# A fused sliding-window attention and gated MLP: plain values loaded once, masks and first keys reordered, plain scores in one visit

## The chip, the cores and the metric

The kernel runs on one core of a Trainium2 chip. The metric is the device time of one execution, in microseconds (us). Before the change the median of four runs is 305.04 us (304.75 to 305.53). One of the executions was taken by the hardware profiler; its own time is 304.69 us.

## The reference

Inputs are q, k and v of shape 8 x 8 x 576 x 64 (batch, head, position, width) and the weights of an MLP: w_in 512 x 2048, w_out 2048 x 512 and beta of 2048. The computation, cut to what matters:

```python
rel = pos[:, None] - pos[None, :]
plain = (rel >= 0) & (rel < 32)                       # heads 0 to 3
dil = (rel >= 0) & (rel < 128) & (rel % 4 == 0)       # heads 4 to 7
attn = softmax(where(mask, q @ k.T / 8, -1e9))
x = concat_heads(attn @ v).reshape(4608, 512)
h = x @ w_in
out = (h * sigmoid(beta * h)) @ w_out
```

So half of the heads attend to the last 32 positions ("plain"), the other half to every fourth of the last 128 ("dilated").

## The kernel before, in words

**Two kinds of work on TensorE.** Attention runs batch by batch (b = 0 to 7), the MLP token tile by token tile (nine tiles of 512 tokens). Per tile there are 16 blocks of h (L811: four matmuls of 512 columns each, then tanh on ScalarE at L820 and the product on VectorE at L825), and four blocks of output (L846: 16 matmuls each, taken in parts of four). Attention of batch b is laid between the MLP matmuls of earlier tiles, because tile t needs the attention of its tokens first.

**The planner.** No order is written by hand. Each step is an `Op` with the engines that may do it, estimated durations, what it depends on and a due number `vt`; `Plan.run` walks through time, and for each engine takes, among the steps that could start within a few tens of ns of the earliest one (`NEAR`), the one with the smallest `vt`. It also hands out the eight PSUM banks: a `Group` of a kind holds a bank until its last reader is done, and `CAPS` says how many a kind may hold (h 3, p 4, o 2, z 4, a 8, s 5). Where PE would stand idle for over 300 ns of planned time it puts in a filler matmul (L958, on zeros). The instruction streams of the engines are fixed by this plan; on the chip each engine follows its own stream in order.

**Plain scores.** The 576 queries of a head are cut into six blocks of 96; a block needs 128 keys (32 before it and its own 96). Two heads sit in the two halves of the 128 partitions, so one matmul uses 64 rows (L673). For batches 0 and 1 a visit to these 64-row matmuls covers one head pair x and half of the blocks (steps S00, S10, S01, S11: 6 matmuls, two banks); from batch 2 on two head pairs together (12 matmuls, four banks, `PAIRED`). An exponential on ScalarE (L576) writes the bank to `pt` (288 columns), and, from batch 1 on, a product with a 0/1 mask on VectorE or GpSimd (L580) zeroes what lies outside the window. In batch 0 the mask is added in PSUM instead: inside the same step the matmuls L631 (dilated, 512 columns) or L661 and L664 (plain) put 0 or -65536 into the bank, and the scores add to it. Values are multiplied at L729, from `pt` and `vp`.

**Plain values.** `vp` holds for each of the 24 blocks all 128 keys with their values, so the 32 rows that two neighbouring blocks share are loaded twice: per batch one DMA of 128 x 24 x 64 (three DMAs for batch 0), issued by GpSimd at L384.

**Loads.** GpSimd issues all loads that change float32 to bf16. At the start these are in order: keys and queries of the dilated heads of batch 0, keys and queries of the plain heads, `vd` (dilated values), `vp` (plain values), then w_in in three chunks of 512, 512 and 1024 columns, the tail values `vt`, keys and queries of batch 1, w_out in two halves and so on. For batches 0 to 2 keys and queries are transposed on TensorE (L448 dilated, L455 plain) and copied out of PSUM (L232); from batch 3 on by DMA transposes that SyncE issues. SyncE's first DMA is `beta_row`, 8 KB. The vector w of halved beta is built by a small transpose (L894).

**Masks.** GpSimd builds them with memsets and affine selects: `add_d`, `add_P`, `add_F` early, `mask_d`, `maskn_PP` and `maskn_FP` (128 x 384 each) later.

Of the kernel before, what the change touches and what calls it, by code (L numbers as in the profile page):

```python
# [22 lines left out]
class Op:  # L23
    def __init__(self, engs, fn, deps, vt, acquire, group, dma, lat, halves=False, sbuf=False):
        self.halves, self.sbuf = halves, sbuf
        self.engs, self.fn, self.vt, self.acquire = engs, fn, vt, acquire
        self.deps = [d for d in deps if d is not None]
        self.dma, self.lat, self.group = dma, lat, group
        self.end = self.ready = None
        self.waits = 0  # L30
        self.next = []
        for g in group if isinstance(group, list) else [] if group is None else [group]:
            g.users.append(self)


class Plan:
# [3 lines left out]
    CAPS = {"h": 3, "p": 4, "o": 2, "z": 4, "a": 8, "s": 5}  # L40
    SWITCH = 95
    LAT = {"PE": 210, "ACT": 45, "DVE": 45, "POOL": 60, "SP": 0}
# [5 lines left out]
    def op(self, engs, fn, deps=(), vt=0.0, acquire=None, group=None, dma=0, lat=None, halves=False, sbuf=False):  # L48
        acquire = acquire if acquire is None or isinstance(acquire, list) else [acquire]
        o = Op(engs, fn, deps, vt, acquire, group or acquire, dma, lat, halves, sbuf)  # L50
        self.ops.append(o)
        return o

    def run(self, filler=None, filler_until=0.0):
# [36 lines left out]
        while n_left:  # L91
# [21 lines left out]
            for e, c in near.items():  # L113
                first = min(s for s, _, _ in c)
                s, o, d = min((x for x in c if x[0] <= first + self.NEAR[e]), key=lambda x: (x[1].vt, x[0]))
                picks.append((s, o.vt, e, o, d))
# [58 lines left out]
def kernel(  # L175
# [38 lines left out]
    APART = 4  # L214

# [26 lines left out]
    mask_n = {n: const([P, 2, 2, QT], BF16, f"maskn_{n}") for n in ("FP", "PP")}  # L242
# [12 lines left out]
    pt = [const([P, NI * 2, P], BF16, f"pt{x}") for x in range(2)]  # L255
# [52 lines left out]
    def t_fill2(e):  # L308
        for x in range(2):
            nc.vector.memset(pt[x][:, :, QT:P], 0.0)  # L310
        nc.vector.memset(ptt[:], 0.0)
    fill2 = plan.op([("DVE", 1500)], t_fill2, vt=-7.9)

    def t_fill3(e):
        nc.vector.memset(vp[0][:, :, D:D + 1], 1.0)
        nc.vector.memset(vp[0][0:WIN, 0, 0:D], 0.0)
# [55 lines left out]
    def first_rows(m):  # L372
        nc.gpsimd.memset(m[0:WIN, 0], 0.0)
    for i, n in enumerate(("PP", "FP")):
        def t_mask_n(e, n=n):
            band(mask_n[n][:].rearrange("p a b n -> p (a b) n"), [[0, 4]], [(1, QT)], WIN, -1, 1.0, 0.0)
            if n == "FP":
                first_rows(mask_n[n])
        late_mask("n" + n, 1900, t_mask_n, -7.183 + .001 * i)
# [17 lines left out]
    def plain_v(b, p0, c0):  # L397
        return bass.AP(tensor=v.tensor, offset=v[b, 0].offset + (p0 - WIN) * D + c0 * QT * D,
                       ap=[[D, P - WIN if p0 else WIN if c0 == 1 else P], [QT * D, 4 * NI - c0], [1, D]])

    def direct_vp(b, deps, vt):
        if b:
            return [load("POOL", (vp[b % 2][:, :, 0:D], plain_v(b, 0, 0)), deps, vt, 768, .27, 1450,
                         1100 if b < DIRECT else 4000)]
        half = 2 * NI
        return [load("POOL", (vp[0][WIN:P, 0:half, 0:D], plain_v(0, WIN, 0)[:, 0:half]), deps, vt, 288, .25),
                load("POOL", (vp[0][0:WIN, 1:half, 0:D], plain_v(0, 0, 1)[:, 0:half - 1]), deps, vt, 92, .25),
                load("POOL", (vp[0][:, half:, 0:D], plain_v(0, 0, half)), deps, vt, 384, .27)]

    def direct_vd(b, deps, vt, tdeps=()):  # L410
        src = v[b, 4:8].rearrange("h (t T) d -> t h (T d)", T=C)[0:P]
        out = [load("POOL", (vd16_of[b].rearrange("p h T d -> p h (T d)"), src), deps, vt, 512, .35)]
        for c in range(2):
            src = bass.AP(tensor=v.tensor, offset=v[b, 4].offset + ((P - WIN) * C + c) * D,
                          ap=[[2 * D, 2 * KTL], [S * D, 4], [1, D]])
            out.append(load("POOL", (vt_[b % 2][:, c, :, 0:D], src), list(tdeps), vt + (1.245 if b == 0 else .02 if b < DIRECT else 0) + .001 + .001 * c, 96, .2))
# [26 lines left out]
    def t_transposes(g, z, kind, i):  # L443
# [6 lines left out]
        else:  # L450
            tp = bank(g, BF16)[:, 0:S].rearrange("p (j g) -> p j g", j=RP)
            for j in range(RP):
                for h in range(2):
                    rows = slice(64 * h, 64 * h + 64)
                    nc.tensor.transpose(tp[rows, j], stp[z][rows, i, j * D:(j + 1) * D], ident_b[rows, rows])  # L455

# [49 lines left out]
    def attention(b, ld, names, vts):  # L506
# [4 lines left out]
        if b < DIRECT:  # L511
            for n in [x for x in names if x[0] in "KQ"]:
# [3 lines left out]
                src = ld["qk", z, 0 if kind == "P" else 4]  # L516
                tr = plan.op([("PE", (18 * mm(64) if kind == "P" else 6 * mm(QT)))],
                             lambda e, g=g, z=z, kind=kind, i=i: t_transposes(g, z, kind, i),
                             [src, ident], vt, acquire=g)
# [40 lines left out]
        vdeps["P", 1] = [ld["vp"][-1], (fill3, fill4)[kv]]  # L560
        vdeps["P", 0] = (ld["vp"][:-1] or ld["vp"]) + [(fill3, fill4)[kv]]
# [11 lines left out]
        def exp_and_mask(key, sop, g, vt, n, sc, w, m, tiles):  # L573
# [4 lines left out]
            if b >= ADDED or key == ("T",):  # L578
                def mask(e):
                    E[e].tensor_tensor(out=w(), in0=w(), in1=m(), op=ALU.mult)  # L580
                ex = plan.op([("POOL", 170 + 2.2 * n), ("DVE", 160 + .8 * n)], mask,
                             [ex] + ([mask_tail] if key == ("T",) else [mask_ops["D"]] if key[0] >= 2 else
                                     [mask_ops["n" + ("PP" if key[1] else "FP")]]), vt, sbuf=True)
# [17 lines left out]
        for name in [n for n in names if n[0] in "ST"]:  # L601
# [24 lines left out]
            if x >= 2:  # L626

                def score(e, xs=xs, gs=gs):
                    if b < ADDED:
                        for g in gs:  # L630
                            nc.tensor.matmul(  # L631
                                bank(g).rearrange("p (a n) -> p a n", a=4), lhsT=ident_b[:],
                                rhs=add_d[:].unsqueeze(1).to_broadcast([P, 4, P]), start=True, stop=False)
                    for n, x in enumerate(xs):
                        for i in range(4):
                            r, h4 = i // 2, 2 * (x - 2) + i % 2
                            for c in range(2):
# [5 lines left out]
                sop = plan.op([("PE", len(xs) * 4 * mm(P) + (190 + 2 * mm(4 * P) if b < ADDED else 0))], score,  # L643
                              deps + ([ident, adds["D"]] if b < ADDED else []), vt, acquire=gs, halves=True)
# [9 lines left out]
            j = int(name[2])  # L654

            def score(e, xs=xs, j=j, gs=gs):
                if b < ADDED:
                    for g in gs:
                        lo = 0
                        if j == 0:  # L660
                            nc.tensor.matmul(bank(g)[:, 0:QT], lhsT=ident_b[:], rhs=add_p["F"][:],  # L661
                                             start=True, stop=False)
                            lo = 1
                        nc.tensor.matmul(  # L664
                            bank(g)[:, lo * QT:3 * QT].rearrange("p (a n) -> p a n", n=QT), lhsT=ident_b[:],
                            rhs=add_p["P"][:].unsqueeze(1).to_broadcast([P, 3 - lo, QT]),
                            start=j == 1, stop=False)
                for n, x in enumerate(xs):
                    for a in range(3):
                        i = 3 * j + a  # L670
                        for h in range(2):
# [4 lines left out]
            sop = plan.op([("PE", len(xs) * 3 * mm(QT) + (190 + 2 * mm(3 * QT) if b < ADDED else 0))], score,  # L676
                          ([o for x in xs for o in steps[f"KP{x}"] + steps[f"QP{x}"]] if b < DIRECT else ready["P"])
                          + ([ident, adds["P"]] if b < ADDED else []), vt, acquire=gs, halves=True)
# [3 lines left out]
            for n, x in enumerate(xs):  # L682
                for h in range(2):
# [4 lines left out]
                                 lambda j=j: mask_n["PP" if j else "FP"][:].rearrange("p a b n -> p (a b) n")[  # L688
                                     :, (0, 1)[j == 0]:(0, 1)[j == 0] + 3],
                                 [("pt", x, i) for i in range(3 * j, 3 * j + 3)])  # L690
        for name in [n for n in names if n[0] in "VU"]:
# [33 lines left out]
            def values(e, x=x, j=j, g=g):  # L725
                pv = bank(g)[:, 0:6 * (D + 1)].rearrange("p (m h e) -> p m h e", m=3, h=2)
                for a in range(3):
                    for h2 in range(2):
                        nc.tensor.matmul(pv[:, a, h2, :], lhsT=pt[x][:, (3 * j + a) * 2 + h2],  # L729
                                         rhs=vp[kv][:, (2 * x + h2) * NI + 3 * j + a, 0:D + 1],  # L730
                                         start=True, stop=True)
            vop = plan.op([("PE", 6 * mm(D + 1))], values,
                          [sdone[x, j, 0], sdone[x, j, 1]]
                          + vdeps["P", x], vt, acquire=g)
            used(("vp", kv), vop)
            for i in range(3 * j, 3 * j + 3):
                used(("pt", x, i), vop)
# [135 lines left out]
    for n, (z, h0) in enumerate(((0, 4), (1, 4), (0, 0), (1, 0))):  # L873
        ld[0]["qk", z, h0] = direct_qk(0, z, h0, [], -9 + .01 * n)
# [27 lines left out]
    vts[first.index("T"):len(first)] = [-.5, -.4, -.3, -.2]  # L902
# [89 lines left out]
```

## Time and profile before

| what | before |
|---|---|
| median of 4 runs | 305.04 us |
| the profiled execution: its time, its span | 304.69 us, 302.8 us |
| PE busy | 293.1 us, 97% |
| VectorE, ScalarE, GpSimd busy | 183.5, 170.9, 90.5 us |
| matmuls with w_in (L811) and w_out (L846) | 138.3 and 139.4 us busy |
| packets of DMA on GpSimd's queue | 66672, 66.1% of the engines' span |
| granted TensorE clock | 0.999 |

The span is the time from the first to the last instruction in the profile, and the execution's own time is 1.89 us longer. Busy PE time counts the filler matmuls too, and the ends of matmuls are modelled, so that two groups of matmuls can overlap in the listing: what a group costs is read from its start to the start of the next group. In the listing by time each row gives start, duration, engine, line, operation, output and inputs, the number of instructions, and in square brackets how long the engine was idle before it and what released it.

### The profile page before, as it was taken

How to read it: one execution, taken by the hardware profiler on the slowest of the kernel's cores; microseconds unless marked ns; L12 is line 12 of the kernel's file. 1: busy time of each engine (PE TensorE's matmuls, PEld its weight loads, DVE VectorE, ACT ScalarE, POOL GpSimd, SP SyncE). 2: the span in 40 equal slices, each digit the busy share in tenths (PEclk: the TensorE clock that was granted, in tenths of full speed). 3: DMA queues.
4: the chain of work that ended last, by engine and by line, in shares of the span. 5: the costliest groups of instructions: out<-in, count | busy, mean ns of one | idle time of the engine just before them, and what ended most of it. 6: DMA issues, size and time to landing. Idle time of an engine off the chain costs nothing.

```text
span 302.8 us, 5999 instructions
## 1 busy us (share of the span) xinstructions
PE 293.1 (97%) x2275; PEld 148.4 (49%) x2312; DVE 183.5 (61%) x424; ACT 170.9 (56%) x314; POOL 90.5 (30%) x131
## 2 busy tenths in 40 slices
PE   7899999999999999999999999999999999999995
PEld 5565545554544444445444444444444444444454
DVE  3568874987866746886676658756764343343300
ACT  2767963877547645765664557555664544554311
POOL 8988562836045106320470055100000000000000
PEclk9999999999999999999999999999999999999999
DMA  6999999999999997999899989996132100100122
GB/s 101 178 210 203 206 184 210 195 128 168 193 181 209 158 209 156 174 122 234 150 165 183 185 185 151 164 191 169 56 93 75 38 35 35 37 35 35 55 83 73
DMA packets 117376, 42.47 MB, mean 140 GB/s; under 512 B 93748, under 2 KB 110916, under 8 KB 117348
## 3 DMA queue, kind: packets, MB, share of 16 engines
q0 software_dynamic: 66672, 19.66, 66.1%
q1 hardware_dynamic: 50532, 22.36, 37.8%
q8 instruction: 18, 0.29, 0.4%
q10 hardware_dynamic: 144, 0.07, 0.1%
q14 instruction: 10, 0.08, 0.1%
HBM read 39.32 MB, written 18.87 MB: 192 GB/s over the span
## 4 chain that ended last, share of the span: by engine, by line
PE 80%; DMA 12%; DVE 3%; issue 2%; POOL 1%; ACT 1%; POOLq 0%; SPq 0%; DVEq 0%
PE bank L846 39%; PE bank L811 34%; DMA vd<-in_v_dram 4%; DMA dk<-s 3%; DMA st<-in_q_dram 2%; PE bank L729 2%; DMA s<-in_k_dram 2%; DVE g L825 1%; PE bank L673 1%; PE bank L639 1%; PE bank L714 1%; POOL st L384 1%; PE bank L699 0%; DVE xdm L596 0%; PE bank L780 0%
## 5 line engine op out<-in xcount | busy, mean ns | idle before, releaser
L846 PE MATMUL bank<-w_out_bf,g 128*128 128x512 bf16 (+2 forms) x587 | 139.4, 367 | 1.7 <-issue 0.8
L825 DVE SCALAR_TENSOR_TENSOR g<-tnh,bank 128x512 bf16<-128x512 bf16 x144 | 97.8, 685 | 70.8 <-ACT tnh L820 69.8
L820 ACT ACTIVATE tnh<-bank,beta_half 128x512 bf16<-128x512 f32 x144 | 98.4, 689 | 72.5 <-PE bank L811 67.0
L811 PE MATMUL bank<-xT,w_in_bf 128*128 128x512 bf16 (+1 forms) x568 | 138.3, 376 | 0.9 <-issue 0.2
L811 PEld LDWEIGHTS <-w_in_bf 128*128 128x128 bf16 x584 | 55.1, 98 | 61.0 <-issue 0.2
L846 PEld LDWEIGHTS <-g 128*128 128x128 bf16 x608 | 54.5, 98 | 55.4
L861 ACT ACTIVATE osb<-bank 128x512 f32<-128x512 f32 (+1 forms) x35 | 20.6, 588 | 31.6 <-PE bank L846 31.3
L576 ACT ACTIVATE pt<-bank 128x288 bf16<-128x288 f32 x64 | 21.5, 418 | 6.3 <-PE bank L673 6.2
L576 ACT ACTIVATE ptd<-bank 128x512 bf16<-128x512 f32 x32 | 16.9, 603 | 7.0 <-PE bank L639 7.0
L596 DVE TENSOR_TENSOR xsp<-bank,rcp 96x384 bf16<-96x384 f32 x32 | 17.7, 554 | 1.1
L384 POOL DMA_DIRECT2D vp<-in_v_dram x10 | 18.0, 1800 | 0.5 <-PE bank L455 0.5
L924 POOL COPY pace<-xT 1x2 bf16<-1x2 bf16 x4 | 0.7, 176 | 58.3 <-DMA xT<-x 58.3
L595 DVE RECIPROCAL rcp<-bank 128x4 f32<-128x4 f32 (+2 forms) x72 | 12.9, 179 | 5.3 <-PE bank L729 3.9
L580 DVE TENSOR_TENSOR ptd<-ptd,mask_d 128x512 bf16<-128x512 bf16 x27 | 12.0, 453 | 6.1 <-ACT ptd L576 4.9
L596 DVE TENSOR_TENSOR xdm<-bank,rcp 128x256 bf16<-128x256 f32 x32 | 13.6, 425 | 1.1
L384 POOL DMA_DIRECT2D vt<-in_v_dram x16 | 13.8, 1048 | 0.0
L384 POOL DMA_DIRECT2D s<-in_q_dram x10 | 13.7, 1370 | 0.0
L729 PEld LDWEIGHTS <-pt 128*128 128x128 bf16 x192 | 9.0, 97 | 5.8 <-POOL pt L580 0.6
L384 POOL DMA_DIRECT2D s<-in_k_dram x10 | 11.2, 1121 | 1.2 <-issue 1.2
L232 POOL COPY vd<-st 128x1024 bf16<-128x1024 bf16 x5 | 5.2, 1036 | 19.0 <-DMA st<-in_v_dram 15.1
L729 PE MATMUL bank<-vp,pt 128*128 128x65 bf16 x192 | 10.1, 193 | 0.1
L863 DVE TENSOR_SCALAR osb<-bank 128x512 f32<-128x512 f32 (+2 forms) x3 | 1.4, 469 | 13.3 <-PE bank L846 13.3
(107 smaller groups left out, 182.7 us busy)
## 6 DMA issues: line engine op xcount, KB each, us to landing
out_dram<-osb SPq DMA_DIRECT2D x35, 256.0 KB, 3.0
s<-in_k_dram POOLq DMA_DIRECT2D x10, 288.0 KB, 6.5
s<-in_q_dram POOLq DMA_DIRECT2D x10, 288.0 KB, 9.4
vp<-in_v_dram POOLq DMA_DIRECT2D x7, 384.0 KB, 18.2
w_out_bf<-in_moe_w_out_dram POOLq DMA_DIRECT2D x2, 1024.0 KB, 16.4
st<-in_k_dram POOLq DMA_DIRECT2D x6, 288.0 KB, 13.1
st<-in_q_dram POOLq DMA_DIRECT2D x6, 288.0 KB, 12.5
x<-xsp SPq DMA_DIRECT2D x12, 144.0 KB
```

Of the source, the lines that this page charges most:

```text
L232: (nc.scalar.copy if e == "ACT" else E[e].tensor_copy)(out=out, in_=in_)
L384: {"POOL": nc.gpsimd, "SP": nc.sync}[queue].dma_start(out=out, in_=in_)
L576: nc.scalar.activation(out=w(), in_=sc(), func=ACT.Exp, scale=SCALE)
L580: E[e].tensor_tensor(out=w(), in0=w(), in1=m(), op=ALU.mult)
L595: nc.vector.reciprocal(out=r, in_=p[..., D])
L596: nc.vector.tensor_tensor(out=dst, in0=p[..., 0:D], in1=r.unsqueeze(len(p.shape) - 1).to_broadcast(list(p.shape[:-1]) + [D]), op=ALU.mult)
L729: nc.tensor.matmul(pv[:, a, h2, :], lhsT=pt[x][:, (3 * j + a) * 2 + h2], rhs=vp[kv][:, (2 * x + h2) * NI + 3 * j + a, 0:D + 1], start=True ...
L811: nc.tensor.matmul(bank(g)[:, a:z], lhsT=w_in_bf[:, kt, fb * P:(fb + 1) * P], rhs=xT[:, kt, xo + a:xo + z], start=(i == 0 and kt == kts[0] ...
L820: nc.scalar.activation(out=th[:, 0:n], in_=bank(g)[:, 0:n], func=ACT.Tanh, scale=beta_half[:, fb:fb + 1])
L825: nc.vector.scalar_tensor_tensor(out=g_t[t % 2][:, fb, c0:c0 + n], in0=th[:, 0:n], scalar=1.0, in1=bank(g)[:, 0:n], op0=ALU.add, op1=ALU.mult)
L846: nc.tensor.matmul(bank(g)[:, lo:hi], lhsT=g_t[t % 2][:, fb, tb * P:(tb + 1) * P], rhs=w_out_bf[:, fb, lo:hi], start=(fb == 0), stop=(fb = ...
L861: nc.scalar.mul(out=ob[:, lo:hi], in_=bank(g)[:, lo:hi], mul=0.5)
```

## The change

Seven edits:

1. `vp` is loaded without the doubled rows: 96 x 24 x 64 per batch into partitions 32 to 127 (two DMAs for batch 0), and the 32 shared rows are copied inside SBUF by VectorE or GpSimd (`halo`: one copy of 32 x 4 x 5 x 64 per batch, two halves for batch 0). The rows that have no predecessor are zeroed once.
2. The additive masks of batch 0 become steps of their own, `added`, which take the banks; the scores follow later.
3. The dilated keys of batch 0 are loaded by SyncE as float32 into the unused `g_t[1]`, and ScalarE and VectorE cast one half each.
4. From batch 3 on all plain scores of a batch are one visit: 24 matmuls into six banks of a new kind "w", six exponentials of 384 columns instead of eight of 288, and six mask products.
5. `maskn_PP` and `maskn_FP` become one `mask_n` of 128 x 864.
6. `vt` of batch 0 and the tail steps of batch 0 get later due numbers.
7. `NUDGE`: 29 steps, by their number, get a bias in ns that shifts the start time by which the planner compares them (it does not shift the step itself).

```diff
+    CAPS = {"h": 3, "p": 4, "o": 2, "z": 4, "a": 8, "s": 5, "w": 6}
+    NUDGE = {75: 400, 116: -150, 160: -150, 200: -400, 206: -900, 210: 400, 221: 60, 240: -60, 250: -150,
...
-                first = min(s for s, _, _ in c)
-                s, o, d = min((x for x in c if x[0] <= first + self.NEAR[e]), key=lambda x: (x[1].vt, x[0]))
+                first = min(s + o.bias for s, o, _ in c)
+                s, o, d = min((x for x in c if x[0] + x[1].bias <= first + self.NEAR[e]), key=lambda x: (x[1].vt, x[0]))
...
+        o = load("SP", (stage, src), [], -9.1, 576, .41, 400, 1200)
+        return [plan.op([("ACT", 175 + .834 * RD * D), ("DVE", 160 + 1.042 * RD * D)],
+                        lambda e, x=x: copy(e, std[0][:, x], stage[:, x]), [o], -9.1, sbuf=True) for x in range(2)]
...
+            o = load("POOL", (vp[b % 2][WIN:P, hs.start * NI:hs.stop * NI, 0:D], src), deps, vt, n * 144, .27,
+                     1150 if b else 750, 1100 if b < DIRECT else 4000)
+            def halo(e, hs=hs):
+                copy(e, rows[0:WIN, hs, 1:NI, 0:D], rows[QT:P, hs, 0:NI - 1, 0:D])
...
+                before = [plan.op([("PE", 2 * mm(4 * P))], added, [ident, adds["D"]], vt, acquire=gs)] if b < ADDED else []
...
+            if b >= AT_ONCE:
+                gs = [Group("w") for _ in range(6)]
...
+                sop = plan.op([("PE", 2 * NI * mm(QT))], score, [o for x in range(2) for o in steps[f"KP{x}"] + steps[f"QP{x}"]]
+                              if b < DIRECT else ready["P"], vt, acquire=gs, halves=True)
...
-    vts[first.index("T"):len(first)] = [-.5, -.4, -.3, -.2]
+    vts[first.index("T"):len(first)] = [.2,.35,.45,.5]
```

In the built programs the streams change as follows. Both have the same matmuls apart from fillers: 35 before, 29 after. TensorE: the four L631 matmuls now stand ahead of the first transposes; the transposes of the plain keys of batch 1 (2 x 18) stand ahead of the first h block, where before they came after the eleventh h block; the runs of 64-row matmuls (transposes L455 and scores, with nothing else between) are 29 instead of 30: five fewer in batches 3 to 7, two more in batch 1, two more in batch 2. GpSimd: the first DMA is now the dilated queries; the plain keys of batch 1 are loaded before the second and third chunk of w_in instead of after. VectorE: both copies of qT of batch 0 and two halo copies stand ahead of the first normalisation (L595); ScalarE casts its half of the keys first, and has two copies of kT of batch 1 ahead of its last xT copy of batch 0. The last 100 output matmuls are the same.

## The prediction

> **What bounds the kernel now.** The first page is read first: TensorE (PE) is busy for 97% of the span. That includes fillers, so the next view is the list of instructions by time. I read it by the distance from the start of one group to the start of the next; the durations themselves overlap.
>
> ```profile
> 1.13 4.43 PE L958 MATMUL bank<-zero 128*128 128x256 bf16 x22 [1.13 <-DVE warm L290]
> 6.06 0.68 PE L448 MATMUL bank<-ident_b,st 96*128 96x96 bf16 x12 [0.50 <-DMA st<-in_k_dram]
> 7.59 0.67 PE L448 MATMUL bank<-ident_b,st 96*128 96x96 bf16 x12 [0.30 <-DVE dk L232]
> ...
> 9.11 0.60 PE L631 MATMUL bank<-add_d,ident_b 128*128 128x512 bf16 x2 [0.41 <-DVE dq L232]
> 9.65 0.40 PE L639 MATMUL bank<-dq,dk 64*128 64x128 bf16 x8
> 9.98 0.76 PE L455 MATMUL bank<-ident_b,st 64*64 64x64 bf16 x36
> 11.36 0.76 PE L455 MATMUL bank<-ident_b,st 64*64 64x64 bf16 x36 [0.63 <-DMA st<-in_q_dram]
> 12.71 0.43 DVE L232 COPY vd<-vd 128x1024 bf16<-128x1024 bf16 x1 [1.18 <-DMA vd<-in_v_dram]
> 13.02 1.08 ACT L576 ACTIVATE ptd<-bank 128x512 bf16<-128x512 f32 x2
> 13.91 0.18 DVE L595 RECIPROCAL rcp<-bank 128x4 f32<-128x4 f32 x1 [0.77 <-PE bank L714]
> 20.14 4.88 PE L811 MATMUL bank<-xT,w_in_bf 128*128 128x512 bf16 x28
> ```
>
> The reader is to see three phases in the first 20 us. Until 11.4 PE waits for loads: keys at 6.06, queries 1.5 us later, the plain queries at 11.36. From 13 to 20.7 it is paced by ScalarE (back to back from 10.08 to 15.8) and VectorE (from 13.91 to 19.9). Then h runs. Lost PE time before the first h block at 18.36: 1.13, 4.93 (to 6.06), 1.01 (6.58 to 7.59), 1.01 (8.10 to 9.11), 0.69 (36 transposes take 1.38 at 9.98, but 0.69 at 11.36), 0.12 of filler, and 0.9 in pieces of 0.1 to 0.24 between 14.3 and 18.2: 9.8 us in all, of which about 6 are the wait for the first load.
>
> The same reading from 18.4 to 60 us gives 1.9 us lost: 0.40 of filler at 24.85, 0.5 at L699 (8 matmuls take 0.75 at 26.18, 0.24 at 48.15), 0.30 and 0.11 around 32, 0.15 at 33.3, 0.26 at 39.8, 0.2 at 56.4. After 60 us four matmuls of 512 columns take 0.86 us again and again; one wait of 0.3 us at 71 is left. So after 60 us only the cost of changing between 128-row and 64-row matmuls can be saved:
>
> ```profile
> 67.40 1.03 PE L846 MATMUL bank<-w_out_bf,g 128*128 128x512 bf16 x4
> 68.36 0.43 PE L673 MATMUL bank<-qT,kT 64*128 64x96 bf16 x12
> 68.72 1.04 PE L846 MATMUL bank<-w_out_bf,g 128*128 128x512 bf16 x4
> 69.59 1.03 PE L811 MATMUL bank<-xT,w_in_bf 128*128 128x512 bf16 x4
> ```
>
> The four ahead of the visit take 0.96 instead of 0.86: 0.10 to enter. Twelve score matmuls take 0.36, six (at 34.51) take 0.24: 0.02 each and 0.12 to leave. A visit costs 0.22 us beyond its work.
>
> **The parts.** All against the profiled execution (304.69, span 302.8).
>
> *Additive masks ahead.* The two L631 pairs take 0.54 each (9.11 to 9.65, 12.05 to 12.59). They move into the wait for the keys: `add_d` is ready at 5.72 now, and one GpSimd issue of 0.79 less stands ahead of it, so about 4.9. The four take 0.86 there, where five of 22 fillers go. That is 1.1 us off PE between 9 and 12.6. All four dilated exponentials can now run before the plain queries are there; today the second pair starts at 13.02. The L661 and L664 masks stay where they are, at 0.04 to 0.17 each.
>
> *Keys by SyncE.* SyncE issues at 0.81, GpSimd at 1.36 with 0.79 per issue. By window, the DMA engines are busy 0.01 of the first 2 us, 0.25 from 2 to 3, 0.78 from 3 to 4: there is room. The queries become GpSimd's first load. They land no earlier than today's first load (6.05) and no later than today (7.54): 0 to 1.5 us for all that follows on that queue. I take 1.0, since the room ahead of 4 us is about one load. The keys themselves: no load of this size stands on SyncE's queue; the nearest rows are a 256 KB store, 3.0 us to landing, and today's first load, 4.7 us, so 3.8 to 5.5; plus the casts (0.64 us on ScalarE and 0.76 on VectorE for 576 elements, by 768/576: 0.85 and 1.0) they are ready at 4.8 to 6.5 against 6.06. Both engines idle there. If they come at 6.5, the queries come next anyway.
>
> A rule speaks against this edit: the Trainium skill, "DMA: Bandwidth & Descriptors", section "Issuing engines are not separate DMA queues", says that issuing from several engines saves only the issuing time, because all queues share the same 16 DMA engines. By it this part would give about 0.8 us, the one issue, and not 1.0; the windows above show the shared engines idle at that time, which the rule doesn't speak of.
>
> *Values.* A quarter of the rows goes: 6144 of 66672 packets over the run. At the start a load of 288 KB lands 1.5 us behind the one before it, and `vp` with w_in's first chunk takes from 12.7 to about 18.1 (issue 10.80, 7.3 to landing): a quarter of `vp` is 0.5 to 0.75 us, take 0.6. Against it stand the halo copies. At the start two of 640 elements, 0.2 to 0.43 each by VectorE's copies of 128 (0.21) and 1024 elements (0.43). They wait for `vp` on VectorE, and behind them all L595/L596 pairs are queued, for which the transposes back (L765, L780) and then h wait. `vp`'s last piece lands today at 14 to 15.5 (issues from 6.45 to 9.0, 6.6 to 7.2 to landing); less 1.0 and 0.6, 12.5 to 13.9; with a copy, L595 starts at 12.8 to 14.3 against 13.91. From there 6.8 us of VectorE work lead to the last x copy (13.91 to 20.74), as now. So the gain of both edits above mostly ends here, as a shorter wait and not as an earlier h. This is the new late thing. Later halo copies (0.3 to 0.6 us each, one per batch) lie beside PE on engines that are 61% and 30% busy, and cost nothing; if VectorE were the bound, they would cost 4 us.
>
> *Plain keys of batch 1 first.* They now stand ahead of chunks two and three of w_in. Today w_in's first chunk lands at 18.1; less 1.6, plus one load of 1.5: these keys land at 18.0, before x is complete at 20.7. Their 36 transposes (0.69 us at 30.84) move into PE's pieces of waiting, 0.9 us: a gain of 0.7. The last chunk of w_in lands today at 25.7 (13.4 and 12.3): minus 1.6 plus 1.5, unchanged.
>
> *Start in sum:* -0.8: the 0.7 and 0.1 from the rest. Its ends: -2.3, if 1.0 of the masks and loads and half of the halo's cover come through; +0.8, if VectorE starts 0.4 later and the keys miss the gaps by as much.
>
> *18 to 60 us.* Fillers are still three after the burst of h. 1.9 us are to be had at most. The loads of batch 1 come at the same time or up to 1.6 earlier. I take -0.4, with ends of -1.5 and +1.0 (the three steps in which batch 1 waits for loads, each once more).
>
> *One visit.* In batches 3 to 7 five visits go, 1.1 us; in batches 1 and 2 four are added, 0.9. Net -0.2. Six exponentials of 384 columns replace eight of 288: 8 x 0.42 = 3.3 against 6 x 0.50 = 3.0 (0.50 between the rows of 288, 0.418, and 512, 0.603), on ScalarE, 56% busy: nothing. The visit must hold six of eight banks at once: from nothing to one tanh and one product (0.69 + 0.69) per visit; I take nothing, as mostly output matmuls stand around it, which stay in one bank for 16 matmuls.
>
> *Mask building* (one of 864 columns instead of two of 384) is GpSimd work at 21 us; the masks are used from about 34 us. Nothing. *The shifts* are in the order that all of the above was read from.
>
> Sum: -0.8 - 0.4 - 0.2 = -1.4, so 303.3 for an execution like the profiled one. That one lies 0.35 below the median, so **303.6 us**, own range 302.8 to 304.4.
>
> **Rivals.**
>
> *The start comes through as well* (18%). If `vp` lands at 12.5, VectorE starts 1.1 earlier and x and h follow: -2.3 at the start, -0.6 later, -0.2: 301.9. For it: all loads shift. Against it: VectorE's chain from 13.9 has no gaps of note and gets more work.
>
> *Nothing comes of it* (15%). The transposes ahead cost as much as the pieces they fill, loads set the pace to 44 us as now: -0.2, 304.8. For it: transposes of batch 1 stand at 27.88, 29.36, 30.84 and 32.16, one load apart, so loads feed PE there.
>
> *Slower by the order of the loads* (10%). The plain keys of batch 1 push w_in's last chunk back by 1.5 us. PE takes the first block of it at 26.93. If SyncE's early start and the lighter `vp` give less than 0.3 together, it lands at 26.9 or later and decides; with no shift at all it lands at 27.2, the dilated keys behind it at 28.7, which now stand ahead of that block in PE's stream: 1.8 lost, less 0.7 and 0.2: 305.9.
>
> *Slower by the banks* (12%). Each of the five visits waits for its sixth bank: 0.5 us, about a third of tanh plus product, is +2.5: 306.1. It decides from 0.3 us per visit on. For it: batch 5 has an h block right ahead of the visit. Against it: PE waits for no bank after 60 us today.
>
> **Chances.** 0.45 forecast, 0.18, 0.15, 0.10, 0.12. Faster by over 0.2% (0.6 us, about what a measurement of this kernel can tell from no change) 0.63, within 0.15, slower 0.22. The range reaches from the better case to the bank case: 301.8 to 306.0.
>
> **What would show it.** Right: the dilated query transposes start at 6.1 to 7.0; L595 first at 12.8 to 14.3; the burst of 28 h matmuls near 20 us with the 36 transposes ahead of it; visits of 24 at 0.60 us with 0.86-us groups around them. Wrong: idle PE before the dilated keys of batch 1 near 27 us; a gap or a long group ahead of a visit of 24; the first L595 after 14.5.

## The result and the profile after

The changed kernel takes **305.62 us** (median of 46 executions, 303.75 to 309.06), the kernel before 305.0 (67 executions, 304.17 to 305.99): a ratio of **1.0021**, 95% interval 1.0012 to 1.0031. The forecast was 303.6. The profiled execution of the changed kernel takes 305.05 us with a span of 303.2, against 304.69 and 302.8 before: 0.4 us more in the span. The changed kernel also spreads over 5 us, the kernel before over 2. The medians here and below count every execution; the ratios leave out the few that lie more than 1.5% above the fastest one of the same kernel, two of the 46 here.

The listing by time of the changed kernel, first 25 us (start, duration, engine, line, operation; its lines are 10 to 60 higher than before: L448 is L467, L455 L474, L595 L620, L811 L869, L846 L904):

```profile
5.22 1.77 PE L655 MATMUL bank<-add_d,ident_b 128*128 128x512 bf16 x4 [0.28 <-POOL add_d L342]
6.94 0.68 PE L467 MATMUL bank<-ident_b,st 96*128 96x96 bf16 x12
7.67 0.83 PE L467 MATMUL bank<-ident_b,st 96*128 96x96 bf16 x12
9.59 0.23 PE L952 MATMUL bank<-ident_f,beta_row 16*128 16x16 f32 x1 [0.66 <-POOL ident_f masks.py:199]
9.75 0.76 PE L474 MATMUL bank<-ident_b,st 64*64 64x64 bf16 x36
...
13.64 0.62 DVE L240 COPY vp<-vp 32x640 bf16<-32x640 bf16 x2
14.19 0.16 DVE L620 RECIPROCAL rcp<-bank 128x4 f32<-128x4 f32 x1
17.64 0.47 PE L474 MATMUL bank<-ident_b,st 64*64 64x64 bf16 x18
...
20.49 4.87 PE L869 MATMUL bank<-xT,w_in_bf 128*128 128x512 bf16 x28
```

The reader is to see that the masks are ahead (5.22) and the transposes of batch 1 too (17.64), but that the dilated queries are transposed no earlier than before (7.67; 7.59 before), the first normalisation neither (14.19; 13.91), and the burst of 28 h matmuls starts 0.35 later (20.49; 20.14), with 36 transposes more behind it. The loads themselves did come earlier: plain keys, plain queries and `vd` land at 8.67, 10.09 and 11.47, against 9.92, 11.32 and 12.69 before, and the last piece of `vp` at 13.35 against 15.20.

The new visit of 24, in the same view:

```profile
84.02 1.24 PE L904 MATMUL bank<-w_out_bf,g 128*128 128x512 bf16 x5
85.19 0.68 PE L693 MATMUL bank<-qT,kT 64*128 64x96 bf16 x24
85.81 1.90 PE L904 MATMUL bank<-w_out_bf,g 128*128 128x512 bf16 x8
```

From start to start it takes 0.62, and the five matmuls ahead take 1.17 instead of 1.08: one entry of about 0.1, and no wait for a bank.

**Where the time went.** To compare equal work I add up, from the listing, what TensorE's work so far costs when nothing waits (0.2155 us per matmul of 512 columns, and so on for each form), and take it from the start of each group: the rest is TensorE's loss, fillers included. At the same points of the work, in us:

| near | 21 us | 33 us | 64 us | 101 us | 152 us | end |
|---|---|---|---|---|---|---|
| before | 9.0 | 10.8 | 11.9 | 12.2 | 12.3 | 12.3 |
| changed | 8.8 | 9.1 | 9.7 | 10.9 | 12.5 | 12.9 |

By 64 us the changed kernel has lost 2.2 us less, more than the forecast's 1.2 for that stretch. (Its four added visits up to there, 0.9 us at the forecast's 0.22 each, count as work here; on the clock it is about 1.3 us ahead.) Then it loses 3.2 us, and the kernel before 0.4. The losses are three: 1.15 us at 73, 1.55 at 140, 0.4 at 188. The work itself (span less loss) is 0.2 us cheaper, 290.3 against 290.5. The listing of the changed kernel at the first two places, GpSimd and VectorE with TensorE behind them:

```profile
68.29 0.54 POOL L240 COPY dkt<-dk 128x384 bf16<-128x384 bf16 x1 [2.24 <-DMA dk<-s]
71.74 0.29 POOL L240 COPY qt<-dq 64x128 bf16<-64x128 bf16 x1 [2.91 <-DMA dq<-s]
72.12 1.57 POOL L605 TENSOR_TENSOR pt<-pt,mask_n 128x288 bf16<-128x288 bf16 x2
...
73.74 0.33 PE L786 MATMUL bank<-vp,pt 128*128 128x65 bf16 x5 [0.48 <-POOL pt L605]
...
138.72 0.48 DVE L240 COPY vp<-vp 32x1280 bf16<-32x1280 bf16 x1 [2.69 <-DMA vp<-in_v_dram]
139.23 0.76 DVE L605 TENSOR_TENSOR ptd<-ptd,mask_d 128x512 bf16<-128x512 bf16 x2
...
139.72 0.30 PE L770 MATMUL bank<-vd,ptd 128*128 128x65 bf16 x4 [0.91 <-ACT ptt L601]
...
141.19 0.28 PE L770 MATMUL bank<-vd,ptd 128*128 128x65 bf16 x4 [0.32 <-DVE xdm L621]
```

At 73 us GpSimd stands in a copy for batch 3 that waits 2.91 us for a load; two masks of batch 2, which TensorE needs now, are queued behind it. At 139 us VectorE stands in the new halo copy of batch 5, which waits 2.69 us for `vp`; the dilated masks are queued behind it. (At 139.72 the profile names ScalarE's exponential of `ptt`, which these matmuls do not read; what they read is `ptd`, masked by VectorE from 139.23 on.) The chain of waits says the same:

```profile
60.89 10.73 DMA dq<-s
71.74 0.30 POOL qt L240
72.12 1.58 POOL pt L605 x2
73.74 0.33 PE bank L786 x5
...
120.06 18.56 DMA vp<-in_v_dram
138.72 0.48 DVE vp L240
139.23 0.76 DVE ptd L605 x2
```

The third place is smaller: two masks of batch 6 on GpSimd, beside four on VectorE that take 3.02 us (0.75 each; six in 2.27 at 86 us).

### The profile page after: what moved, and what is told of

Same layout as the page of the kernel before. It is cut to its first block, busy times and chain, and to the rows that moved or that the text cites. A ratio compares the mean times of both kernels' runs of the same rounds, so it can differ in the third digit from the quotient of the medians.

```text
span 303.2 us, 5971 instructions
## 1 busy us (share of the span) xinstructions
PE 292.0 (96%) x2269; PEld 149.7 (49%) x2306; DVE 187.0 (62%) x426; ACT 170.1 (56%) x302; POOL 87.9 (29%) x128
## 4 chain that ended last, share of the span: by engine, by line
PE 77%; DMA 14%; POOL 3%; DVE 3%; issue 2%; POOLq 0%; DVEq 0%
PE bank L904 37%; PE bank L869 31%; DMA vp<-in_v_dram 6%; DMA st<-in_k_dram 4%; DMA dq<-s 4%; PE bank L786 1%; PE bank L665 1%; PE bank L770 1%; PE bank L693 1%; DVE pt L605 1%; PE bank L467 1%; POOL st L391 1%; PE bank L474 1%; PE bank L655 1%; PE bank L755 1%
## 5 line engine op out<-in xcount | busy, mean ns | idle before, releaser
L904 PE MATMUL bank<-w_out_bf,g 128*128 128x512 bf16 (+2 forms) x587 | 136.9, 367 | 2.1 <-issue 1.3
L869 PE MATMUL bank<-xT,w_in_bf 128*128 128x512 bf16 (+1 forms) x568 | 136.5, 376 | 0.8
L869 PEld LDWEIGHTS <-w_in_bf 128*128 128x128 bf16 x584 | 55.1, 98 | 61.1 <-issue 0.2
L904 PEld LDWEIGHTS <-g 128*128 128x128 bf16 x608 | 55.0, 98 | 57.0
L601 ACT ACTIVATE pt<-bank 128x384 bf16<-128x384 f32 (+1 forms) x54 | 20.4, 467 | 5.4 <-PE bank L693 3.6
L605 DVE TENSOR_TENSOR pt<-pt,mask_n 128x384 bf16<-128x384 bf16 (+1 forms) x40 | 14.9, 402 | 5.0 <-ACT pt L601 4.6
L620 DVE RECIPROCAL rcp<-bank 128x4 f32<-128x4 f32 (+2 forms) x72 | 12.9, 179 | 5.5 <-PE bank L786 2.9
L391 POOL DMA_DIRECT2D vp<-in_v_dram x9 | 15.2, 1688 | 1.2 <-DVE pt L605 0.7
L605 DVE TENSOR_TENSOR ptd<-ptd,mask_d 128x512 bf16<-128x512 bf16 x28 | 11.3, 423 | 5.0 <-ACT ptd L601 4.3
L391 POOL DMA_DIRECT2D s<-in_q_dram x10 | 13.3, 1334 | 0.0
L391 POOL DMA_DIRECT2D vt<-in_v_dram x16 | 13.3, 986 | 0.0
L391 POOL DMA_DIRECT2D s<-in_k_dram x10 | 11.1, 1113 | 1.3 <-issue 0.9
L786 PE MATMUL bank<-vp,pt 128*128 128x65 bf16 x192 | 10.6, 193 | 0.9 <-POOL pt L605 0.8
L921 DVE TENSOR_SCALAR osb<-bank 128x512 f32<-128x512 f32 (+2 forms) x4 | 2.1, 523 | 14.0 <-PE bank L904 14.0
## 6 DMA issues: line engine op xcount, KB each, us to landing
st<-in_k_dram POOLq DMA_DIRECT2D x5, 288.0 KB, 12.9
```

Source lines behind the costliest of these rows:

```text
L391: {"POOL": nc.gpsimd, "SP": nc.sync}[queue].dma_start(out=out, in_=in_)
L601: nc.scalar.activation(out=w(), in_=sc(), func=ACT.Exp, scale=SCALE)
L620: nc.vector.reciprocal(out=r, in_=p[..., D])
L786: nc.tensor.matmul(pv[:, a, h2, :], lhsT=lhs, rhs=vp[kv][:, (2 * x + h2) * NI + 3 * j + a, 0:D + 1], start=True, stop=True)
L869: nc.tensor.matmul(bank(g)[:, a:z], lhsT=w_in_bf[:, kt, fb * P:(fb + 1) * P], rhs=xT[:, kt, xo + a:xo + z], start=(i == 0 and kt == kts[0] ...
L904: nc.tensor.matmul(bank(g)[:, lo:hi], lhsT=g_t[t % 2][:, fb, tb * P:(tb + 1) * P], rhs=w_out_bf[:, fb, lo:hi], start=(fb == 0), stop=(fb = ...
```

## The experiments

Theory: the start gives its lead, and copies that wait for a load at the head of an in-order engine take it back. Rivals: the lead cannot be kept, since some other late transfer shows as soon as one wait is gone; or the start itself gives nothing. Most kernels take the planner's order of the changed kernel as a list (`self.log`) and move entries of it before anything is issued; the rest of every stream stays. For e4, e7 and e8 the planner ran anew; in e7 its order came out the same, in e8 it differs in the first 25 us. The runs were made on several chips, where the kernel before has medians from 304.72 to 305.32; each ratio is to the kernel before on the same chip, so kernels of different rows are best compared by their ratios.

| kernel | median us (runs) | ratio to before, 95% | loss at 21, 33, 64, 101, 152 us, end |
|---|---|---|---|
| changed | 305.62 (46) | 1.0021 (1.0012 to 1.0031) | 8.8, 9.1, 9.7, 10.9, 12.5, 12.9 |
| e1 halo late | 307.17 (6) | 1.0078 (1.0054 to 1.0103) | 9.2, 9.5, 10.1, 11.3, 13.4, 14.9 |
| e2 masks first | 305.2 (12) | 1.0005 (0.9985 to 1.0026) | 9.1, 9.4, 10.9, 10.9, 12.8, 13.2 |
| e3 both | 306.25 (12) | 1.0033 (1.0007 to 1.0059) | 9.3, 9.6, 10.2, 10.2, 10.9, 12.2 |
| e4 no shifts | 306.68 (6) | 1.006 (1.0036 to 1.0084) | 9.2, 10.9, 11.7, 14.5, 14.6, 14.7 |
| e5 copy 5 moved | 303.81 (12) | 0.9953 (0.9933 to 0.9972) | 9.3, 9.6, 11.2, 11.3, 11.4, 12.0 |
| e6 masks 6 | 303.69 (12) | 0.9951 (0.993 to 0.9971) | 9.5, 9.8, 11.4, 11.4, 11.5, 11.8 |
| e7 doubled again | 304.65 (12) | 0.998 (0.9956 to 1.0005) | 9.3, 9.6, 11.1, 12.4, 14.0, 14.1 |
| e8 keys by GpSimd | 307.25 (6) | 1.007 (1.0045 to 1.0095) | 10.6, 10.9, 12.6, 13.3, 15.1, 15.5 |
| e9 copy on ScalarE | 303.78 (8) | 0.9961 (0.9947 to 0.9974) | 9.7, 10.0, 10.7, 10.8, 10.9, 11.6 |
| e10 changed again | 306.78 (12) | 1.0053 (1.0032 to 1.0075) | 9.8, 10.1, 10.7, 13.2, 15.0, 15.5 |
| e11 fillers | 304.95 (12) | 0.9995 (0.998 to 1.001) | 9.2, 9.5, 11.1, 11.1, 12.5, 12.9 |
| e12 all | 303.45 (8) | 0.9948 (0.9929 to 0.9967) | 9.1, 9.4, 10.3, 10.3, 10.5, 11.1 |

**e1: the halo copies of batches 4 to 7 right ahead of their use.**

```diff
+        for b in range(4, 8):
+            i = next(i for i, (o, e) in enumerate(self.log) if o and o.label == ("halo", b))
+            x = self.log.pop(i)
+            j = next(j for j, (o, e) in enumerate(self.log) if o and o.label == ("vP", b))
+            self.log.insert(j, x)
```

> The changed kernel's plan, emitted from a list, with one edit: in batches 4 to 7 the halo copy stands on VectorE right ahead of the batch's first value matmul in the list, not ahead of the dilated masks. Theory A (two steps that wait for DMAs hold up an in-order queue after 60 us): the 1.5 us lost at 138 to 141 us goes, median 304.1 (303.6 to 304.8), and the spread of the runs shrinks. Theory B (the six-bank visits and the changed start are what costs): no change, 305.6. Theory C (the wait comes back at the value matmuls, because vp is late there too): PE waits at the first value matmul of batch 5, 305.2 to 305.6.

Slower. The step at 140 us is gone, but a copy right ahead of its use is on the path itself, at 122 us (+2.2) and 190 us (+1.5). In this kernel's listing by time:

```profile
120.77 2.23 POOL L402 DMA_DIRECT2D vp<-in_v_dram  x1
...
120.27 1.97 DVE L251 COPY vp<-vp 32x1280 bf16<-32x1280 bf16 x1
...
122.29 0.47 PE L801 MATMUL bank<-vp,pt 128*128 128x65 bf16 x10 [1.77 <-DVE vp L251]
```

The same copy takes 1.97 us, not 0.48, beside GpSimd's DMA issues. The place was wrong, not the theory.

**e2: on GpSimd, masks of batch 2 ahead of the copies for batch 3.**

```diff
+        late = [x for x in self.log if x[0] and x[1] == "POOL" and x[0].label in (("dkt", 3), ("qt", 3))]
+        last = [x for x in self.log if x[0] and x[1] == "POOL" and x[0].label[:2] == ("mask", 2)][-1]
...
+        self.log[j:j] = first
```

> The changed kernel's plan with one other edit: on GpSimd the two copies of batch 3 that wait for DMA transposes (dkt, the first half of qt) stand behind the two plain masks of batch 2 instead of ahead of them. Theory A: the 1.15 us lost at 72 to 74 us goes, median 304.5 (304.0 to 305.0). Theory B: 305.6. Theory C (the copies are now late for the tail scores of batch 3): a wait at the tail scores near 77 us, 305.2 to 305.6.

The step at 73 us is gone, the one at 140 stays (+1.35, +0.49); a new one of 0.9 at 58.7 appears in this execution. The median falls by 0.4, within the interval of no difference.

**e3: e1 and e2 together.**

> Both edits together. Theory A: the two losses add, 1.5 + 1.15 = 2.65 off: 303.0 (302.6 to 303.6), below the kernel before, with no PE wait over 0.5 us after 60 us. Theory B: 305.6.

Its profiled execution (304.27) has 10.2 at 101 us and 10.9 at 152, then loses 1.1 at 188, where the late copy is on the path; the median is no better. Four of its twelve executions show a mean clock of 0.994 and take 306.8 to 308.7; the other eight have a median of 305.5, still far above the expected 303.0. A miss for the move of e1 again.

**e4: no shifts** (`NUDGE = {}`).

> The changed kernel with an empty table of shifts; the planner then orders freely. Theory A: the two queue waits come from where the planner puts copies that wait for DMAs, which the table moves about by chance; the start up to 60 us stays about 2 us ahead of before, and later waits of 0 to 4 us come at other places: 303 to 307. Theory D (the shifts are what makes the start faster): loses 1 us or more by 60 us, 306 to 308.

This is the outcome of theory D. Without the shifts the loss at 33 us is 10.9, as before the change, and another 2 us go at 74. The lead from 21 to 33 us comes with the shifts: without them the plain keys of batch 1 are loaded behind w_in's second and third chunk again and transposed at 29.25, not at 17.64. The wait at 74 is the one behind GpSimd's copies (3.20 us for the load, here too).

**e5: e2, and only the halo copy of batch 5 moved**, to the idle time ahead of that batch's plain masks.

```diff
+        x = next(x for x in self.log if x[0] and x[0].label == ("halo", 5))
+        self.log.remove(x)
+        j = next(j for j, (o, e) in enumerate(self.log) if o and o.label == ("mask", 5, ("P", 0)))
+        j = [i for i in range(j) if self.log[i][0] and self.log[i][1] == "DVE"][-1]
+        self.log.insert(j, x)
```

> Two moves within the changed kernel, nothing else: on GpSimd the copies of batch 3's dilated operands go behind the two plain masks of batch 2, as in the run with masks first; on VectorE the copy of the value rows of batch 5 goes from ahead of the dilated masks (138.72 us) to the last stretch of idle time ahead of that batch's plain masks (about 151 us; GpSimd has no DMA to issue there, and the load has landed 12 us earlier). Theory 1 (the lead that the start gives is taken back by waits behind copies that stand in order and wait for a load): the steps of +1.15 us at 73 and of +1.07 and +0.48 us at 140 are both gone, the loss of TensorE ends near 10.5 to 11.0 us, and the median lies at 303.0 to 304.0, below the kernel before. Theory 2 (the waits only absorb what some other late transfer would take anyway): the steps move elsewhere, the loss ends at 12 to 13, the median at 305 to 306.

The two places in its profile, the values at 74.11 and 139.03 now right behind the work ahead of them:

```profile
72.38 1.89 PE L892 MATMUL bank<-xT,w_in_bf 128*128 128x512 bf16 x8
74.11 0.34 PE L808 MATMUL bank<-vp,pt 128*128 128x65 bf16 x6
...
138.91 0.28 PE L656 MATMUL bank<-qt,dkt 128*128 128x64 bf16 x4
139.03 0.29 PE L792 MATMUL bank<-vd,ptd 128*128 128x65 bf16 x4
```

Both steps are gone and nothing comes in their place after 64 us: 303.81, 0.5% below the kernel before. This decides between the two theories, for the first. The loss at the end is 1 us above what was expected, for a step of 0.95 at 59.0 (57.19 to 59.02 for four matmuls that take 0.86):

```profile
55.97 1.80 DVE L258 COPY vd<-vd 128x1024 bf16<-128x1024 bf16 x1
...
59.02 1.02 PE L927 MATMUL bank<-w_out_bf,g 128*128 128x512 bf16 x4 [0.79 <-DVE g L906]
```

VectorE's copy of `vd` for batch 2 takes 0.42 us in the changed kernel's profile and 1.66 to 1.82 in six others (e2, e5 to e8, e11); the products queued behind it are late.

**e6: e5, with the masks of batch 6 on VectorE.**

> The run with the copy of batch 5 moved, and the two plain masks of batch 6 that GpSimd makes go to VectorE (six in a row there, as in the other late batches). If two engines that mask at once slow each other, the six take about 2.3 us (as at 86 us of the changed kernel) instead of 3.02 us for four, the values of batch 6 no longer wait near 188 us, and 0.3 to 0.4 us go: 302.7 to 303.7. If VectorE is the late one there, two more masks on it cost 0.4 to 0.8 us: the wait at 188 us grows and the median is 0.3 to 0.8 us above that of the run with the copy moved.

A miss: 303.69 against 303.81 can't be told apart, and the step at 188 us is 0.27 with the masks on VectorE and 0.28 without. Five masks in a row take 2.62 us there; what makes that step stays open.

**e7: doubled rows again for batches 3 to 7.**

```diff
+            if b >= 3:
+                into = vp[b % 2][:, :, 0:D]
+                src = bass.AP(tensor=v.tensor, offset=v[b, 0].offset - WIN * D, ap=[[D, P], [QT * D, 4 * NI], [1, D]])
...
+                if b < 3:
+                    copy(e, rows[0:WIN, hs, 1:NI, 0:D], rows[QT:P, hs, 0:NI - 1, 0:D])
```

> The changed kernel, but the plain values of batches 3 to 7 are loaded with doubled rows again (128 partitions), and there is no copy of rows for them; order otherwise as it was. Theory 1: the step at 140 us (+1.55 us) goes with the copy; the one at 73 us (+1.15 us, behind the dilated copies on GpSimd) stays; loads that are a third larger cost little, as TensorE waits for no plain values after 60 us: loss at the end 11.0 to 11.7, median 304.0 to 304.6. Rival (the smaller load is what holds the lead, the copies are only its price): the loads of the dilated keys and queries, which stand behind these on the queue, land later, new steps of 1 us or more appear ahead of the dilated masks, median 305.5 to 306.5.

304.65, about 1 us below the changed kernel, just above the range expected: the copies cost more than the lighter loads save. The wait at 140 is gone, the one at 73 stays (+1.2). The profiled execution (306.2, well above the median) also waits 1.27 us at 145 for the transposed x; whether the heavier load causes it is open.

**e8: the first keys by GpSimd.** (The numbers of `NUDGE` are moved along with the two steps that go.)

```diff
-        ld[0]["qk", z, h0] = first_keys() if n == 0 else direct_qk(0, z, h0, [], -9 + .01 * n)
+        ld[0]["qk", z, h0] = direct_qk(0, z, h0, [], -9 + .01 * n)
```

> The changed kernel with the first keys loaded by GpSimd again instead of by SyncE; behind 60 us the order is the same, and in the first 25 us some fillers and transposes change places with it. Theory 1 (the issue by SyncE brought almost nothing, as the dilated queries were transposed at 7.67 us against 7.59 before): the keys are transposed near 6.1, the queries near 7.6, the loss at 20 us is 9.0 to 9.6 as in the changed kernel, the median within 0.4 us of its 305.6. Rival (it brought the 0.8 us of one issue, and the rest hid it): the queries come at 8.3 or later, the loss at 20 us is 10.0 or more, the median 306.2 to 306.6.

The rival is right, and more: 1.5 us slower than the changed kernel by the ratios. In its listing by time:

```profile
8.21 0.68 PE L467 MATMUL bank<-ident_b,st 96*128 96x96 bf16 x12 [0.48 <-DMA st<-in_q_dram]
...
19.85 0.47 PE L474 MATMUL bank<-ident_b,st 64*64 64x64 bf16 x18 [1.00 <-DMA st<-in_k_dram]
```

Every load behind it is issued 0.6 later; against the changed kernel the queries land 1.0 later (8.17 against 7.16; they are transposed 0.54 later) and the plain keys of batch 1 2.2 later. So what this edit brought is hidden when the changed kernel is set against the one before, whose queries were transposed at 7.59: GpSimd issued both loads at nearly the same times as in e8 (1.36 and 2.14; 1.37 and 2.21), yet in e8 the keys land at 6.25 instead of 6.01 and the queries at 8.17 instead of 7.49. Why is open.

**e9: e6, with the `vd` copy of batch 2 on ScalarE** behind the four dilated exponentials.

> The run with the masks of batch 6 on VectorE, and one copy more moved: the copy of batch 2's dilated value rows goes from VectorE (where it took 1.69 to 1.82 us near 56 us in five profiled runs, and 0.42 in four others) to ScalarE, behind that batch's four dilated exponentials. Theory (VectorE's copy is held up when it falls beside GpSimd's DMA issues; the products queued behind it come late, and TensorE loses 0.85 us at 59.9): ScalarE's copy takes 1.0 to 1.1 us, VectorE's products come on time, the step at 59.9 us is 0.3 us or less, and the median is 303.0 to 303.4, 0.3 to 0.7 below the run it is made from. Rival (the lead that runs out at 59.9 is load time, the copy only stands where it shows): the step stays at 0.6 or more, or goes to the dilated values at 61 us, and the median stays at 303.7 or rises.

ScalarE's copy takes 1.08 us (1.09 in e12's profile), the step at 59 us is gone from the profile, and the median is where it was, 303.78. By the time alone this is inconclusive. In its profiled execution the granted clock is 0.50 from 10.6 to 14.05 us, the mean 0.993, and it takes 303.75, the median all the same.

**e10: the changed kernel once more.**

> The changed kernel itself once more, to see which of its steps of loss recur from one execution to another. Theory 1: the steps at 73 us and at 140 us are there again within 0.3 us (they stand behind loads in a fixed order), those at 18 us (transposes of batch 1's keys, which wait for their load) and at 59.9 us (VectorE's copy beside GpSimd's issues) come and go, and make most of the spread. Rival: the steps at 73 and 140 come and go as well, so that the loss after 60 us differs by 1 us or more between the two profiled executions.

The places recur and the sizes do not: 1.96 at 73 (1.15 in the first profile), 1.75 at 140 (1.55), 0.6 more at 103, where VectorE's copy of `vd` waits 1.63 us for its load. So the expected "within 0.3" fell; the waits follow their loads, which vary. Its first 15 us differ as well (rows of the table by window: busy time of PE, weight loads, VectorE, ScalarE, GpSimd with the number of instructions; granted clock; DMA share; GB/s):

```profile
8.00:9.00 1.00, 0.46 (x5) 0.17 (x2) 0.90 (x3) 0.44 (x1) 0.79 (x4) 1.00 1.25 198
9.00:10.00 1.00, 0.18 (x3) 0.15 (x3) 0.30 (x2) 0.00 (x0) 0.79 (x5) 1.00 1.40 188
10.00:11.00 1.00, 1.00 (x45) 0.96 (x46) 0.40 (x2) 0.51 (x1) 0.99 (x2) 0.83 2.15 164
11.00:12.00 1.00, 1.00 (x20) 0.71 (x18) 0.54 (x1) 0.82 (x3) 0.93 (x3) 0.50 2.41 155
```

TensorE is thin from 8 to 10 us (it waits 1.36 for `ident_f`), and from 10.7 to 14.1 the granted clock is 0.50.

Two more rows of this profile differ from the first one's (5.22 1.77 and 13.64 0.62):

```profile
5.18 1.02 PE L655 MATMUL bank<-add_d,ident_b 128*128 128x512 bf16 x4 [0.72 <-POOL add_d L342]
...
14.60 1.17 DVE L240 COPY vp<-vp 32x640 bf16<-32x640 bf16 x2
```

The four masks take 0.86 from start to start here and 1.6 in the first profile; the two halo copies take 1.17 instead of 0.62, and the first normalisation starts at 15.70 instead of 14.19.

**e11 and e12: six more fillers ahead of the transposition of beta**, in the changed kernel and in e9.

```diff
+        j = next(j for j, (o, e) in enumerate(self.log) if o and o.label == ("beta",))
+        i = [i for i in range(j) if self.log[i][0] is None][-1]
+        self.log[i:i] = [self.log[i]] * 6
```

> The changed kernel with six more fillers in TensorE's stream, behind the four that stand ahead of the transposition of beta (8.3 to 9.6 us, where TensorE waits for GpSimd's identity and for the plain keys); nothing else. In the repeated run TensorE was busy 0.64 of the 2 us from 8 to 10, and the granted clock was 0.50 from 11 to 14 us; in the first profile of the changed kernel it was busy 1.35 of them, and the clock stayed at 1.00. Theory (the thinner stretch lets the clock fall in some executions): no execution shows a mean clock under 0.998, the slowest ones, 308 and more, are gone, and the median falls by 0.2 to 0.6 against the changed kernel on this chip type (305.6 to 306.8), to 305.2 to 306.2; the steps at 73 and 140 us stay. Rival (late loads make both the idle time and the length; the clock only shows them): clocks of 0.994 go, and the median and the slowest executions stay as they were, 305.6 to 306.8 and over 308.

> The run with the copy of batch 2 on ScalarE (303.78), with the same six fillers. Theory: clocks under 0.998 are gone, the loss at 20 us is 9.3 to 9.5 as in the run with the copy of batch 5 moved, and the median is 303.2 to 303.7, with all executions within 1.5 us. Rival: fillers push the plain keys' transposes back where the keys come early, 0.2 to 0.4 us: 303.8 to 304.2.

With fillers none of 20 executions has a mean clock under 0.998 (before: 4 of 90, changed: 6 of 46, e10: 4 of 12). But e2, e5 and e7 have none in 12 each without them, so that the fillers keep the clock up is likely and not shown. e11 lies at 304.95 with all executions from 304.01 to 305.4: the spread is gone, and 0.7 us of the median. (Its profile has a step of 0.95 at 58.9 in place of the one at 73, which was expected to stay, and the one at 140: 0.77 and 0.48.) e12 adds the four moves: **303.45** (303.06 to 304.06), 0.9948 of before, the lowest median; by their intervals e5, e6, e9 and e12 can't be told apart. Executions of the changed kernel at full clock reach 308.2, and in e6 the three at 0.993 and 0.994 take 303.6 to 305.0, its others 302.6 to 304.9. So the clock isn't the whole of the spread, and what the fillers do for it is open.

## Why the prediction was wrong

The sum has nothing for waits after 60 us, and there the direction went wrong. The sentence that failed is "Later halo copies (0.3 to 0.6 us each, one per batch) lie beside PE on engines that are 61% and 30% busy, and cost nothing", with "So after 60 us only the cost of changing between 128-row and 64-row matmuls can be saved". The duration was right (0.48) and the share of busy time too. But what such a copy costs is not its duration: it waits for a load at the head of an in-order engine, 2.69 us, and the dilated masks stand behind it. Before, `vp` was waited for only by the value matmuls, in batch 5 11 us after it landed (141.49; 152.88). The prediction did this step for the start ("They wait for `vp` on VectorE, and behind them all L595/L596 pairs are queued") and not for batches 1 to 7. This is 1.55 of the 2.8 us below. For the 1.15 at 73 us there is no term at all: the prediction didn't ask what the new order puts behind the copies for batch 3 on GpSimd, which are no halo copies. No rival had these waits.

| term | forecast | in the profiled execution |
|---|---|---|
| start, to 21 us | -0.8 | -0.2 |
| 18 to 60 us | -0.4 | -1.5 from 21 to 33, -0.5 from 33 to 64 |
| visits | -0.2 | -0.2 (work 290.3 against 290.5) |
| waits after 64 us | 0 | +2.8 (3.2 less 0.4 before) |
| sum | -1.4 | about -0.2 - 2.0 - 0.2 + 2.8 = +0.4 |

- *Masks ahead.* They run at 5.22, but the four take 1.6 us, not 0.86, and push the keys' transposes to 6.94, though the keys are cast by 6.33. The price was read from a later place: up to 6.8 us in this execution a matmul of 512 columns takes 0.43 and a filler of 256 columns 0.21, behind it 0.22 and 0.11. Before the change the fillers change from 0.21 to 0.11 at 4.9, and in e9 to e12 at 3.8 to 4.5; there the four masks take 0.86 as forecast, and the queries are transposed at 7.16 to 7.39. The time that the masks left became fillers and idle time from 8.33 to 9.75, where the plain keys are transposed (9.98 before). They had landed at 8.67, but the new order has the transposition of beta ahead of them, which waits for `ident_f` from GpSimd (9.59): again an in-order wait. What it costs in the end no run shows.
- *Keys by SyncE.* The forecast interval for the queries, 6.1 to 7.0, was missed (7.67). Yet undone in the changed kernel this edit costs 1.5 us (e8): it was worth more than forecast, and the size was taken against a start that was 0.6 quicker than the changed kernel would have had without it.
- *Values at the start.* First L620 at 14.19, forecast 12.8 to 14.3, "mostly ends here": right in this profile, and partly luck. Of the eleven profiles with this order on VectorE at the start (all but e4 and e8) four have the two halo copies at 0.62 to 0.71 us and the first L620 at 14.0 to 14.2; in seven the copies take 1.17 to 1.19, and it starts at 14.9 to 15.7, past the 14.5 that was to show the forecast wrong. The other ten have lost 9.1 to 9.8 us at 21 us, more than the 9.0 of before, so the start's -0.2 belongs to the profiled execution.
- *Batch 1's keys ahead.* Right that 36 transposes go into gaps; the gain shows from 21 to 33 us, and was undersized. Without the shifts (e4) it isn't there.
- *One visit.* Right: 0.62 (0.60), no wait for a bank. The rival of the banks is refuted, and so is the one of the load order (idle PE ahead of batch 1's dilated keys is 0.26 at 26.88).
- *Median.* The changed kernel's median lies 0.57 above its profiled execution; the forecast added 0.35. The repeated profile shows an execution with a thin start, slower halo copies and longer waits.

With the waits taken out, the time is near the forecast: 303.81 (e5) and 303.45 (e12) against 303.6. That the sum then fits is partly luck: in e5 the start gives no gain (9.3 against 9.0), the stretch from 21 to 33 us gives more than forecast, a step of 0.95 at 59 us takes part of it back, and e12 has moves and fillers that the forecast didn't have.

## What to carry to other kernels

A copy that follows a load costs its place, not its length: when a change adds one, look up on its engine what stands behind it, and for each batch compare when the load lands with when the next thing behind is due. Put such a copy behind the work that is due first and into idle time ahead of its use, neither where the load is still under way nor right ahead of the reader. And when a kernel gains early and ends where it was, compare both traces at equal work: the lead and the places where it is given back can then be read separately.

## What the runs showed of the hardware

- VectorE's copies beside GpSimd's DMA issues can take about four times as long: 0.42 and 1.66 to 1.82 us for 128 x 1024, 0.48 and 1.97 for 32 x 1280. ScalarE's copy of 128 x 1024 took 1.09 beside the same issues; no run has it without them. The Trainium skill, "SBUF — State Buffer", section "SBUF: two separate sides", says that VectorE in its fast modes and GpSimd lock each other out of a shared pair of ports, and warns of DMAs held up by it; here it is the copy that is held up. Copies that began during an issue also ran in 0.42, so the overlap alone does not decide.
- Masks of 128 x 384 on VectorE take 0.38 us each alone (six in 2.27 at 86 us) and 0.75 while GpSimd copies and masks (four in 3.02 at 185 us).
- At the start matmuls take twice as long, until 3.8 to 6.8 us from one execution to another: 0.21 and then 0.11 us for 256 columns.
- The granted clock fell to 0.50 for 3.4 us behind a stretch in which TensorE was busy 1.35 of 3 us with no gap over 1.36 (e10, 7 to 10 us; e9 the same at 1.39). The Trainium skill, "TensorE: Matmul & The Clock Gate", section "HAM oscillation — how this bites in real kernels", names gaps of over 3.4 us as what lets it fall; here less was enough. At 1.63 us of 3 (e6's profile) the clock stayed; but there the matmuls had become fast at 5.8 us, in e9 and e10 at 3.8, so no threshold follows.
